# Weights cast by GpSimd's DMAs instead of VectorE, with deeper pools and a new assignment of copies to engines, in an attention and channel-mix kernel

## The chip, the cores and the metric

One core of a Trainium2 chip. The time is the device time of one execution in microseconds (us). The kernel before takes 171.91 us (median of 3 runs, 171.80 to 172.16); in the later calls, on other chips, its median was 172.37 to 172.44.

## The reference

Windowed attention with four sink tokens, then a channel mix with a shift by one token:

```python
q, k, v: (4, 8, 768, 64) float32          # batch, heads, tokens, head size
keep = is_sink | ((rel >= 0) & (rel < 128))
a = softmax(where(keep, q @ k.T / 8, -1e9));  x = (a @ v)  # -> (4, 768, 512)
x_prev = x shifted by one token
xk = mu_k * x + (1 - mu_k) * x_prev;   xr = mu_r * x + (1 - mu_r) * x_prev
k = max(xk @ w_k, 0)          # w_k 512 x 1024
v = (k * k) @ w_v             # w_v 1024 x 512
out = v / (1 + exp(-(xr @ w_r)))   # w_r 512 x 512, all float32
```

## The kernel before

The work is cut in 12 units of 256 tokens. A unit loads k, q and v, casts them to bf16, transposes k and q (on TensorE, or for later units by DMA), does scores, exponentials, mask, values, then xk and xr, then the products with wk, wr and wv. Every operation is put in a list; each engine runs its operations in a fixed order (`ORDER`), which a search has tuned. Where the plan expects TensorE to be idle for over 0.3 us at the start it puts filler products ("warm") in. They are instructions like any other and run even when the data come sooner. In the profile's lines ks, qs and vs are the loaded fp32 tiles of k, q and v; kb, qb and vb their bf16 casts; kt and qt the transposes; sc the scores and e their exponentials; rl the relu and kk its square; ob the output tile that a store reads; bank a PSUM tile.

All large transfers go through the one queue of the sync engine (SP), in order: inputs, weights, stores and DMA transposes. Weights arrive in fp32; VectorE casts them (and halves wv):

```python
LOADS = ("kq0", "v0", "kq1", "wka", "v1", "wkb", "wr", "wva", "wvb")   # order of the first loads
...
wk32 = tile1([128, NC, Dff], FP32, "wk32")        # and wr32, wv32
...
P.op("SP", 1000.0, lambda: nc.sync.dma_start(out=dst, in_=src), rank, ...)      # load_weight
...
P.op("DVE", dve(1024, 0.52), (lambda: nc.vector.tensor_scalar(        # cast: 10 of them
    out=out, in0=in_, scalar1=0.5, scalar2=None, op0=ALU.mult)) if half else
    (lambda: nc.vector.tensor_copy(out=out, in_=in_)), ...)
...
for name in ("ks", "qs", "vs"):
    pool(name, 3, [128, 2, H, D] if name == "vs" else [128, H, 2, D], FP32)
KD = range(4, 12); QD = range(8, 12)     # units whose k, q are transposed by DMA
```

The softmax here doesn't subtract the row's maximum and nothing guards it: scores larger than these inputs give would overflow.

Of the kernel before, what the change touches and what calls it, by code (L numbers as in the profile page):

```python
# [8 lines left out]
FP32 = mybir.dt.float32  # L9
# [8 lines left out]
CAST = {"k": "ACT", "q": "ACT"}  # L18

CAST0 = {"k": "DVE", "q": "DVE"}  # L20
EVAC0 = {"k": "ACT", "q": "DVE", "x": "ACT"}

KD = range(4, 12)
QD = range(8, 12)
# [11 lines left out]
LOADS = ("kq0", "v0", "kq1", "wka", "v1", "wkb", "wr", "wva", "wvb")  # L36
WCAST = ("DVE",) * 10
VCAST = ("DVE", "POOL")
# [6 lines left out]
        92, 89, 98, 105, 95, 116, 108, 113, 128, 141, 124, 119, 131, 137, 103, 148, 134, 157,  # L45
        155, 168, 219, 211, 207, 212, 220, 208, 160, 176, 165, 171, 183, 189, 215, 193, 200,
        223, 180, 216, 225, 237, 298, 186, 290, 302, 291, 303, 299, 294, 248, 295, 227, 235,
        231, 263, 232, 228, 260, 306, 266, 318, 240, 256, 245, 251, 310, 276, 269, 311, 283,
        326, 329, 308, 321, 314, 343, 315, 370, 378, 352, 366, 371, 379, 332, 367, 374, 382,
        337, 375, 384, 359, 348, 386, 396, 387, 421, 390, 274, 444, 391, 452, 445, 453, 426,  # L50
        407, 448, 456, 394, 449, 457, 460, 399, 464, 404, 465, 415, 462, 410, 430, 472, 499,
        578, 437, 468, 474, 504, 469, 525, 583, 526, 537, 485, 538, 533, 509, 529, 534, 530,
        477, 553, 482, 488, 493, 545, 511, 564, 518, 549, 541, 546, 543, 550, 601, 609, 605,
        602, 556, 610, 606, 567, 631, 613, 561, 572, 614, 617, 587, 619, 621, 594, 629, 622,
        634, 625, 639, 626, 642, 677, 689, 678, 681, 663, 690, 682, 645, 707, 685, 650, 686,
        695, 701, 670, 718, 705, 702, 693, 697, 710, 698, 760, 715, 761, 756, 768, 757, 769,
        721, 726, 764, 742, 765, 772, 749, 740, 784, 780, 774, 781, 795, 834, 830, 835, 842,
        831, 787, 843, 838, 792, 798, 860, 776, 803, 816, 839, 777, 823, 846, 848, 854, 858,
        855, 871, 910, 918, 906, 911, 907, 850, 863, 851, 919, 868, 936, 874, 914, 879, 915,
        930, 892, 924, 899, 931, 926, 947, 934, 922, 944, 939, 927, 976, 972, 977, 984, 973,  # L60
        985, 950, 980, 955, 958, 981, 988, 990, 965, 992, 996, 993, 997, 1012, 1000, 1013, 1004,
        1001, 1005, 1008, 1016, 1009, 1020, 1018, 1021, 1028, 1024, 1029, 1025,
    ),
    "DVE": (
        70, 91, 88, 93, 97, 71, 94, 99, 100, 107, 112, 101, 123, 109, 114, 110, 118, 115, 120,
        125, 143, 121, 126, 146, 144, 78, 145, 150, 79, 151, 152, 81, 164, 154, 104, 159, 147,
        175, 170, 161, 80, 162, 177, 166, 178, 167, 172, 153, 173, 82, 83, 202, 195, 196, 210,
        69, 197, 203, 204, 198, 206, 84, 85, 205, 199, 214, 218, 239, 293, 301, 222, 86, 305,
        87, 255, 297, 250, 233, 244, 229, 241, 242, 257, 246, 247, 252, 258, 253, 325, 320, 278,
        312, 279, 285, 280, 287, 322, 286, 327, 323, 328, 331, 316, 281, 289, 288, 282, 354,  # L70
        333, 334, 336, 369, 373, 338, 355, 339, 377, 361, 381, 362, 356, 363, 388, 275, 357,
        392, 364, 365, 398, 358, 403, 447, 451, 414, 455, 400, 459, 401, 409, 405, 406, 466,
        416, 417, 411, 412, 432, 433, 434, 439, 441, 440, 435, 470, 442, 481, 476, 528, 436,
        510, 487, 492, 478, 532, 479, 483, 443, 489, 484, 494, 490, 495, 540, 555, 560, 513,
        536, 514, 520, 516, 515, 522, 521, 547, 551, 523, 571, 517, 566, 557, 558, 604, 524,
        568, 569, 562, 563, 573, 574, 608, 633, 612, 616, 589, 592, 590, 638, 623, 635, 591,
        596, 598, 597, 627, 636, 640, 641, 593, 599, 644, 600, 665, 649, 646, 680, 692, 647,
        684, 651, 652, 714, 666, 688, 709, 672, 667, 674, 703, 668, 675, 673, 711, 725, 699,
        712, 676, 716, 720, 669, 717, 722, 723, 727, 759, 728, 763, 744, 767, 745, 751, 771,
        746, 753, 752, 741, 786, 782, 747, 755, 791, 797, 788, 789, 833, 793, 799, 802, 794,  # L80
        800, 748, 804, 845, 805, 754, 837, 778, 841, 825, 818, 821, 819, 820, 826, 829, 827,
        867, 856, 862, 822, 878, 909, 864, 873, 865, 852, 913, 869, 870, 875, 876, 880, 828,
        881, 917, 921, 894, 943, 897, 932, 895, 938, 896, 901, 905, 902, 945, 903, 940, 941,
        928, 949, 946, 954, 904, 951, 952, 898, 956, 975, 957, 960, 979, 961, 963, 987, 962,
        983, 967, 969, 970, 968, 971, 994, 964, 998, 1003, 1007, 1015, 1011, 1022, 1030, 1026,
    ),
    "ACT": (
        67, 68, 90, 111, 106, 96, 122, 117, 127, 130, 136, 142, 129, 132, 133, 149, 138, 163,
        135, 158, 156, 169, 174, 221, 213, 182, 209, 188, 184, 190, 201, 194, 179, 185, 224,
        181, 217, 226, 238, 187, 243, 292, 262, 300, 304, 296, 254, 249, 236, 264, 259, 265,  # L90
        261, 307, 267, 319, 268, 324, 277, 270, 284, 342, 340, 309, 330, 335, 344, 345, 347,
        353, 372, 380, 368, 420, 425, 383, 376, 360, 498, 418, 349, 385, 397, 422, 503, 423,
        402, 496, 454, 427, 446, 413, 450, 395, 458, 408, 461, 501, 577, 582, 575, 463, 431,
        473, 500, 438, 579, 475, 480, 505, 584, 527, 486, 491, 535, 531, 539, 559, 554, 512,
        519, 565, 580, 542, 544, 653, 570, 655, 603, 611, 607, 657, 632, 615, 618, 588, 659,
        637, 630, 620, 731, 595, 735, 643, 648, 679, 664, 691, 683, 729, 713, 708, 687, 671,
        696, 733, 808, 724, 706, 694, 719, 806, 762, 810, 758, 770, 743, 766, 812, 750, 785,
        790, 775, 773, 801, 882, 796, 836, 832, 844, 866, 861, 840, 817, 824, 849, 847, 884,
        859, 888, 886, 872, 877, 912, 908, 942, 920, 916, 893, 937, 925, 900, 935, 948, 923,
        953, 978, 974, 986, 959, 989, 982, 991, 966, 1014, 1002, 1006, 1010, 1019, 1017,  # L100
    ),
    "POOL": (
        77, 72, 73, 75, 76, 74, 102, 139, 140, 191, 192, 271, 273, 272, 350, 351, 428, 506, 429,
        585, 507, 661, 508, 586, 662, 737, 738, 739, 814, 815, 890, 891,
    ),
    "SP": (
        1, 3, 0, 2, 4, 5, 6, 7, 8, 11, 9, 10, 16, 12, 15, 13, 20, 14, 19, 17, 18, 21, 22, 25,
        23, 234, 24, 30, 341, 28, 35, 346, 313, 29, 317, 26, 33, 27, 389, 38, 34, 40, 31, 419,
        424, 36, 393, 497, 230, 32, 502, 37, 41, 43, 576, 39, 467, 44, 45, 581, 46, 47, 656, 42,
        548, 51, 654, 471, 52, 660, 658, 49, 552, 628, 57, 50, 48, 55, 56, 53, 730, 732, 736,  # L110
        58, 734, 54, 704, 61, 807, 811, 809, 813, 63, 700, 783, 64, 624, 62, 883, 59, 60, 885,
        889, 887, 857, 65, 853, 779, 66, 929, 933, 999, 995, 1023, 1031, 1027,
# [4 lines left out]
class Plan:  # L117
# [17 lines left out]
    def op(self, engine, cost, emit, rank, reads=(), writes=(), take=(), hold=(), port=False,  # L135
           lag=None, service=0.0, descs=128, mode=0):
        self.ops.append(dict(engine=engine, cost=cost, emit=emit, rank=rank, reads=list(reads),
                             writes=list(writes), take=list(take), hold=list(hold), port=port,
                             lag=90.0 if lag is None else lag, service=service, descs=descs, mode=mode))

    def schedule(self):
# [42 lines left out]
        while any(lines.values()):  # L184
# [35 lines left out]
            if o["service"]:  # L220

                descs = o["descs"]
# [9 lines left out]
                flying.append((dma, descs))  # L232
# [39 lines left out]
def kernel(  # L272
# [14 lines left out]
    nc = tc.nc  # L287
# [21 lines left out]
    for name in ("ks", "qs", "vs"):  # L309
        pool(name, 3, [128, 2, H, D] if name == "vs" else [128, H, 2, D], FP32)  # L310
    pool("kb", 3, [128, 2, H, D], BF16)
    pool("qb", 3, [128, 2, H, D], BF16)
    pool("kt", 4, [128, NP, 2, 128], BF16)
    pool("qt", 3, [128, NP, 2, 128], BF16)
    pool("e", 5, [128, 2, 512], BF16)
    pool("es", 3, [128, 256], BF16)
    pool("rec", 6, [128, 2, 2, 1], FP32)
    pool("x", 3, [128, 2, Dm], BF16)
    pool("td", 3, [128, 2, 256], BF16)
    pool("xk", 3, [128, NC, 256], BF16)  # L320
    pool("xr", 3, [128, NC, 256], BF16)
    pool("kk", 2, [128, NF, 256], BF16)
# [85 lines left out]
    for u in range(2, U):  # L408
        load(u, "kqv", -90 if u == 2 else 10 * u - 18)
# [521 lines left out]
```

## Time and profile before

| | before |
|---|---|
| time, median | 171.91 us |
| TensorE (PE) busy | 161.4 us of a span of 169.9 (95%) |
| VectorE (DVE), ScalarE (ACT), GpSimd (POOL) busy | 149.4, 132.5, 25.1 us |
| first product with wk / wr / wv starts | 21.30 / 28.79 / 36.85 us |

The first products mark the end of the head: from 36.85 on TensorE has all it needs. The "body" below is the stretch from the first wv product to the start of the last group of products (164.80 in this kernel, so 127.95 us). The timeline of the sync engine's issues shows the head's order of transfers (start, time until the next issue, engine and line, what, count):

```profile
8.21 2.38 SPq L397 DMA_DIRECT2D wk<-in_moe_w_k_dram  x2
10.64 4.65 SPq L360 DMA_DIRECT2D vs<-in_v_dram  x2
15.33 3.32 SPq L377 DMA_DIRECT2D qs<-in_q_dram  x1
18.69 1.82 SPq L397 DMA_DIRECT2D wr<-in_moe_w_r_dram  x1
21.25 1.51 SPq L397 DMA_DIRECT2D wv<-in_moe_w_v_dram  x1
24.02 4.44 SPq L397 DMA_DIRECT2D wv<-in_moe_w_v_dram  x1
```

The reader is to see that wk goes ahead of v of unit 1, but wr and wv go behind it: one queue, in the order in which the data are wanted. The landings follow: v of unit 1 at about 22, wr at 26.8.

### The profile page before, as it was taken

The numbers are of one execution on the slowest core, as the hardware profiler recorded it, in microseconds if no ns is written. First come the engines' busy times: TensorE is split into PE (matmuls) and PEld (weight loads), VectorE is DVE, ScalarE is ACT, GpSimd is POOL, SyncE is SP. The second block draws the span as 40 slices with busy tenths as digits, with TensorE's granted clock in tenths as the row PEclk, the third lists the DMA queues.
The fourth block names the chain that finished last, engine by engine and source line by source line (L and its number), as shares of the span: only waits on it lengthen the run. The fifth ranks groups of instructions, "written<-read, shape, count | busy, mean of one in ns | idle before, by whom it ended". The sixth has DMA issues, their size and how long they took to land.

```text
span 169.9 us, 4214 instructions
## 1 busy us (share of the span) xinstructions
PE 161.4 (95%) x1603; PEld 107.9 (63%) x1624; DVE 149.4 (88%) x372; ACT 132.5 (78%) x219; POOL 25.1 (15%) x47
## 2 busy tenths in 40 slices
PE   7898998999999999999999999999999999999992
PEld 2445575675768567768567677577585775684751
DVE  2588999999899788899999999998999999999632
ACT  3179987999999999999878979978887938654330
POOL 6130030006200030124201200110200403000000
PEclk9999999999999999999999999999999999999999
DMA  4999999999959899999858998999989974030203
GB/s 113 254 283 385 277 279 342 353 268 211 287 142 222 228 254 254 172 234 192 208 130 121 268 233 199 227 115 233 164 237 169 186 215 130 0 127 0 112 11 123
DMA packets 82803, 33.82 MB, mean 199 GB/s; under 512 B 64736, under 2 KB 77280, under 8 KB 82784
## 3 DMA queue, kind: packets, MB, share of 16 engines
q1 hardware_dynamic: 81728, 33.56, 86.8%
q8 instruction: 12, 0.20, 0.5%
q10 hardware_dynamic: 1056, 0.00, 0.3%
q14 instruction: 7, 0.06, 0.1%
HBM read 24.12 MB, written 6.29 MB: 179 GB/s over the span
## 4 chain that ended last, share of the span: by engine, by line
PE 81%; DVE 6%; DMA 5%; SPq 4%; issue 1%; ACT 1%; DVEq 0%
PE bank L818 24%; PE bank L859 23%; PE bank L841 12%; PE sc L635 6%; PE bank L694 6%; DMA wk<-in_moe_w_k_dram 5%; PE bank L733 3%; SPq L377 3%; PE bank L550 2%; PE bank L682 2%; PE bank L611 2%; SPq L360 1%; DVE e L671 1%; DVE wk_sb L503 1%; PE bank L788 1%
## 5 line engine op out<-in xcount | busy, mean ns | idle before, releaser
L818 PE MATMUL bank<-xk,wk_sb 128*128 128x256 bf16 x384 | 48.9, 273 | 0.0
L657 ACT ACTIVATE e<-sc 128x1024 bf16<-128x1024 f32 (+1 forms) x48 | 45.0, 975 | 4.9 <-PE sc L635 4.9
L859 PE MATMUL bank<-wv_h,kk 128*128 128x512 bf16 x173 | 45.3, 379 | 0.6
L818 PEld LDWEIGHTS <-wk_sb 128*128 128x128 bf16 x384 | 35.7, 98 | 7.1 <-issue 0.2
L575 POOL CAST vb<-vs 128x512 bf16<-128x512 f32 x22 | 18.4, 845 | 111.4 <-DMA vs<-in_v_dram 101.4
L827 ACT ACTIVATE rl<-bank 128x512 bf16<-128x512 f32 x48 | 27.6, 608 | 9.1 <-PE bank L818 8.4
L671 DVE TENSOR_TENSOR e<-e,mask 128x1024 bf16<-128x1024 bf16 (+1 forms) x48 | 31.6, 669 | 0.4 <-ACT e L657 0.4
L859 PEld LDWEIGHTS <-kk 128*128 128x128 bf16 x184 | 16.6, 98 | 14.7 <-DVE kk L831 0.3
L841 PE MATMUL bank<-wr_sb,xr 128*128 128x512 bf16 x88 | 23.9, 379 | 0.8 <-DVE wr_sb L503 0.4
L831 DVE TENSOR_TENSOR kk<-rl 128x512 bf16<-128x512 bf16 x48 | 20.9, 447 | 4.1 <-ACT rl L827 3.9
L768 DVE SCALAR_TENSOR_TENSOR xr<-td,mu,xt 128x256 bf16<-128x256 bf16 x48 | 23.2, 499 | 0.1
L768 DVE SCALAR_TENSOR_TENSOR xk<-td,mu,xt 128x256 bf16<-128x256 bf16 x48 | 22.3, 491 | 0.2
L710 DVE TENSOR_TENSOR x<-bank,rec 128x256 bf16<-128x256 f32 x48 | 19.5, 417 | 0.6
L694 PE MATMUL bank<-vb,e 128*128 128x65 bf16 x352 | 18.9, 193 | 0.4 <-DVE e L671 0.4
L694 PEld LDWEIGHTS <-e 128*128 128x128 bf16 x352 | 16.7, 97 | 2.8 <-DVE e L671 0.6
L847 ACT ACTIVATE th<-bank 128x512 f32<-128x512 f32 x24 | 14.1, 602 | 5.0 <-PE bank L841 4.8
L868 DVE SCALAR_TENSOR_TENSOR ob<-th,bank 128x512 f32<-128x512 f32 x23 | 15.7, 682 | 2.1 <-ACT th L847 1.7
L744 ACT COPY xt<-bank 128x512 bf16<-128x512 bf16 x24 | 14.1, 592 | 4.1 <-PE bank L733 3.8
L841 PEld LDWEIGHTS <-xr 128*128 128x128 bf16 x96 | 9.0, 98 | 8.2 <-issue 0.4
L635 PE MATMUL sc<-qt,kt 64*128 64x128 bf16 (+1 forms) x256 | 14.0, 238 | 0.0
L879 PE MATMUL bank<-warm 128*128 128x512 bf16 x42 | 12.3, 423 | 1.4 <-DVE warm L894 1.3
L635 PEld LDWEIGHTS <-kt 64*128 64x128 bf16 x256 | 8.9, 94 | 6.1 <-issue 3.7
(54 smaller groups left out, 158.5 us busy)
## 6 DMA issues: line engine op xcount, KB each, us to landing
vs<-in_v_dram SPq DMA_DIRECT2D x24, 256.0 KB, 5.0
out_dram<-ob SPq DMA_DIRECT2D x23, 256.0 KB, 3.4
ks<-in_k_dram SPq DMA_DIRECT2D x18, 256.0 KB, 4.9
qs<-in_q_dram SPq DMA_DIRECT2D x7, 512.0 KB, 6.2
qs<-in_q_dram SPq DMA_DIRECT2D x10, 256.0 KB, 4.1
wk<-in_moe_w_k_dram SPq DMA_DIRECT2D x2, 1024.0 KB, 8.7
wv<-in_moe_w_v_dram SPq DMA_DIRECT2D x2, 1024.0 KB, 12.3
ks<-in_k_dram SPq DMA_DIRECT2D x3, 512.0 KB, 8.1
```

Source lines behind the costliest of these rows:

```text
L575: lambda g=g, copy=copy: copy(out=buf["vb", u][:, g, :, 0:D], in_=buf["v", u][:, g, :, :]), rank,
L635: nc.tensor.matmul(out=sc[:, a, o0:o1], lhsT=lhs[rows], rhs=rhs[rows], start=True, stop=True)
L657: nc.scalar.activation(out=buf[ek][:, :, lo:], in_=buf[sck][:, :, lo:], func=AF.Exp, scale=scale)
L671: nc.vector.tensor_tensor(out=at, in0=at, in1=m, op=ALU.mult)
L694: nc.tensor.matmul(out=o[:, g, a, :], lhsT=e[:, a, e0:e0 + 128], rhs=rhs, start=(T == 0 and i == 0), stop=(i == len(blocks) - 1), skip_gro ...
L710: P.op("DVE", dve(256), lambda ok=ok, rk=rk, c=c: nc.vector.tensor_tensor(out=buf["x", u][:, :, 128 * c:128 * c + 128].rearrange("p g (a d ...
L768: nc.vector.scalar_tensor_tensor(out=buf[key][:, c0 + i, :], in0=buf[tk][:, i, :], scalar=mu[w][:, c0 + i:c0 + i + 1], in1=xt[:, c0 + i, t ...
L818: nc.tensor.matmul(out=ps[:, i, :], lhsT=wk_sb[:, c, 128 * f:128 * f + 128], rhs=xk[:, c, :], start=(c == 0), stop=(c == NC - 1), skip_gro ...
L827: P.op("ACT", act(512), lambda psk=psk, rk=rk: nc.scalar.activation(out=buf[rk], in_=buf[psk].rearrange("p (i t) -> p i t", i=2), func=AF. ...
L831: P.op("DVE", dve(512, 0.52), lambda f2=f2, rk=rk: nc.vector.tensor_tensor(out=buf["kk", u][:, 2 * f2:2 * f2 + 2, :], in0=buf[rk], in1=buf ...
L841: nc.tensor.matmul(out=buf[psk], lhsT=buf["xr", u][:, c, 128 * g:128 * g + 128], rhs=wr_sb[:, c, :], start=(c == 0), stop=(c == NC - 1))
L859: nc.tensor.matmul(out=buf[psk], rhs=wv_h[:, f, :], lhsT=buf["kk", u][:, f, 128 * g:128 * g + 128], start=(f == 0), stop=(f == NF - 1))
```

## The change

The intent: GpSimd's DMAs cast fp32 to bf16 on the way, so the casts of wk and wr on VectorE go away, and the fp32 copies of the weights with them (40 KB of each partition, which deeper pools take). Then the assignment of copies to engines and all orders were searched anew.

```diff
-LOADS = ("kq0", "v0", "kq1", "wka", "v1", "wkb", "wr", "wva", "wvb")
-WCAST = ("DVE",) * 10
+LOADS = ("kq0", "v0", "kq1", "v1")
+WLOADS = (("wk", 0, 2, ("q", 0, 1)), ("wk", 2, 4, ("v", 0, 1)), ("wr", 0, 2, ("k", 1, 1)),
+          ("wv", 0, 2, ("k", 1, 1)), ("wv", 2, 4, ("q", 1, 1)))   # each behind this landing
-QD = range(8, 12)
+QD = range(6, 12)
+CHOICE = {80: "DVE", ...}     # some 60 casts, evacuations, relus: which engine
 ...                           # ORDER: all five lists new
-        P.op("SP", 1000.0, lambda: nc.sync.dma_start(out=dst, in_=src), rank, service=service,
+        def emit():
+            t = buf[what, u]
+            t = t[0:1, part, 0, 0:1] if what == "v" else t[0:1, 4 * part, 0, 0:1]
+            nc.gpsimd.tensor_copy(out=gate[0:1, n:n + 1], in_=t)
+            nc.gpsimd.dma_start(out=dst[cut], in_=src[cut])
 ...
-        pool(name, 3, [128, 2, H, D] if name == "vs" else [128, H, 2, D], FP32)
-    pool("kb", 3, ...); pool("qb", 3, ...); pool("qt", 3, ...); pool("e", 5, ...)
+        pool(name, 4, [128, 2, H, D] if name == "vs" else [128, H, 2, D], FP32)
+    pool("kb", 4, ...); pool("qb", 4, ...); pool("qt", 4, ...); pool("e", 6, ...)   # and others
-    for i in range(4): cast(i, wk_sb..., wk32...)      # and 2 of wr, 4 of wv
+    # only wv is halved, in place, in bf16
```

The copy of one element into `gate` is what makes each weight DMA wait for an input.

## The prediction

> **What bounds the kernel now.** I read the page first: busy shares and the slices, then the chain that ended last.
>
> ```profile
> span 169.9 us, 4214 instructions
> ...
> PE 161.4 (95%) x1603; PEld 107.9 (63%) x1624; DVE 149.4 (88%) x372; ACT 132.5 (78%) x219; POOL 25.1 (15%) x47
> ...
> PE   7898998999999999999999999999999999999992
> ...
> DVE  2588999999899788899999999998999999999632
> ...
> PE 81%; DVE 6%; DMA 5%; SPq 4%; issue 1%; ACT 1%; DVEq 0%
> ```
>
> The reader is to see that TensorE is the bound, that VectorE is close behind it, and that 15% of the final chain is not TensorE: a DMA of wk and its queue (5% + 4%) and VectorE (6%). These must lie at the start, so I took the busy time of each engine in stretches.
>
> ```profile
> 0.00:5.00 5.00, 3.74 (x11) 1.43 (x12) 1.48 (x5) 1.28 (x1) 3.66 (x14) 1.00 0.58 130
> ...
> 15.00:20.00 5.00, 4.19 (x51) 2.70 (x49) 4.59 (x13) 4.95 (x9) 0.00 (x0) 1.00 1.15 324
> ...
> 80.00:100.00 20.00, 19.83 (x212) 12.81 (x211) 19.69 (x53) 16.28 (x29) 3.52 (x6) 1.00 0.85 180
> ...
> 160.00:165.00 5.00, 4.95 (x31) 2.96 (x31) 1.61 (x4) 2.57 (x6) 0.00 (x0) 1.00 0.28 105
> ```
>
> (Columns: stretch, length, then busy us of PE, PE weight load, DVE, ACT, POOL, clock, DMA share, GB/s.) In the middle PE idles under 1% and DVE is 98% busy too: both are full. From 40 to 160 PE's idle time sums to only 1.0 us. PE in the first 20 us looks busy but is not: the timeline shows what it does.
>
> ```profile
> 18.27 0.63 PE L611 MATMUL bank<-qt,ksink 128*128 128x256 bf16 x4
> 18.95 1.72 PE L879 MATMUL bank<-warm 128*128 128x512 bf16 x7
> 20.61 0.76 PE L635 MATMUL sc<-qt,kt 64*128 64x256 bf16 x12
> 21.30 2.79 PE L818 MATMUL bank<-xk,wk_sb 128*128 128x256 bf16 x24
> ```
>
> The warm products are filler. The channel-mix product with wk, the first dense work, starts at 21.30. Real PE work, by the spacing of back-to-back products in the chain (0.109 us for a 256-column one, 0.216 for 512): 384+16 products of 256 columns 43.6, 184+96 of 512 columns 60.4, scores about 10, values with sinks about 14, sink scores 3.5, the 48 groups of four transposes at 0.22 10.6, sink values 0.8: **143 us**. Before 21.30 only some 5 us of it is done (8 groups of transposes, two units' scores, one unit's values). So the time is 21.3 (start) + 145.4 (to the last products at 166.7; 138 of work, some 4.5 of the 0.1 us steps around each group of scores, 2.4 of visible idle) + 3.2 (last eviction and store).
>
> **What sets 21.3** is in the chain in order of time:
>
> ```profile
> 8.21 7.76 DMA wk<-in_moe_w_k_dram
> ...
> 16.01 0.75 DVE x L710 x2
> ...
> 17.55 0.60 DVE wk_sb L503
> 18.16 0.39 DVE xk L768
> ...
> 18.89 0.59 DVE wk_sb L503
> ...
> 19.80 0.48 DVE xk L768
> 20.28 0.60 DVE wk_sb L503
> ```
>
> VectorE ends attention of unit 0, then makes xk and casts wk by turns: 3 x 0.60 = 1.8 us of casts lie on the path, and earlier 1.8 us of memsets (7.83 to 9.7 in its timeline) sit ahead of the second k cast at 9.64.
>
> **What the Trainium skill says.** (1) "DMA: Bandwidth & Descriptors", SWDGE vs HWDGE vs iDMA: a cast during DMA is only possible from GpSimd. So moving weights to that queue is what removes the casts; no run here shows it yet. (2) The same page, Issuing engines are not separate DMA queues: all issuers share 16 engines. The trace agrees in kind: everything but the two mu loads goes through one queue and fills the engines (1.15 of 1 as the view counts it at 15 to 20 us), so the 5 MB of weights still compete with the inputs. (3) "SBUF — State Buffer", SBUF: two separate sides: VectorE in a two-port mode locks GpSimd out, and descriptors for GpSimd's DMAs then come late. The trace has only casts on GpSimd to compare: 0.85 us mean for 128x512, between 0.61 and 1.07, while VectorE is full. (4) "VectorE: DVE Perf Modes", the perf-mode tier table: bf16 copies in SBUF are faster than fp32 ones, and PSUM sources are capped. Agrees: a 128x512 cast in SBUF 0.42, a PSUM copy of the same size 0.72; so halving wv in bf16 should cost less than the 0.687 it costs from fp32. My estimate is 0.35.
>
> **The change part by part.**
>
> *Weight path.* Removed from VectorE: 6 casts x 0.60 spacing = 3.6 us, of which 1.8 lies on the path to 21.3; 4 halvings drop from 0.60 to about 0.28: 1.3. In exchange GpSimd issues five DMAs, each after one landed input. In its order they stand behind a v cast and the sink keys, which need unit 0's kt (before: 11.35 to 12.0). So wk leaves about 10 to 12 us, against 8.21 and 9.4 before, where landing took 7.9 and 9.5. wk lands, I estimate, at 17 to 20 (first half), so it may just meet xk.
>
> *Head order.* Loads now go k, q, q, k; unit 0's first pair is complete with the second landing, not the third (6.4 us in the trace), and the memsets come before the casts. I estimate first scores 0.5 to 1 us sooner than 8.21 and the second pair 1.5 us sooner than 11.34. Against that, VectorE's order puts three more PSUM copies of unit 1 (0.62 each by spacing) before xk, and v's second half queues behind all of k of unit 1. Net with the 1.8 us of casts: the first wk product 1 to 3 us sooner, at **about 19.3**. The instruction lists support it: 44 fillers become 29. At 0.21 us each that is 3.2 us less of gaps that the author's order expects.
>
> *PE.* q of units 6 and 7 is transposed by DMA: 4 groups less, 4 x 0.22 = **0.9 us** off the bound, and 2 more groups come before the first wk product (0.4). Cost: 4 more DMA transposes (3.3 us to landing, hidden).
>
> *VectorE, ACT, GpSimd.* Counting the lists: ACT loses 17 casts of k and q, 10 evacuations, 2 xt and 5 relus, and gains 10 v casts: 17x0.53 + 10x0.65 + 7x0.5 - 10x0.5 = 14 us less. VectorE gains 7 k/q casts and 6 v casts (13x0.35), 8 evacuations and transposed copies (8x0.62) and 5 relus (5x0.6): 12.5 us more, less the 4.9 above: **+7.6**, so some 157 us busy. About 5 of the gains are in the first 20 us, where it has 6.3 us idle. GpSimd swaps 16 v casts for 10 k/q casts: less work. So in the middle VectorE's load stays near 128 of 135 us, since 6 weight operations leave and about 7 us come. It stays full; I book no gain and no loss.
>
> *Deeper pools.* They can only take PE's 2.4 us of visible idle, and most of that is waits on VectorE or ACT at 24 to 30. I book **0.5**.
>
> Sum: 2.0 (start) + 0.9 + 0.5 + about 0.4 (two more groups done early) = 3.8 off 171.9: **168.1**; rounded to **168.0**.
>
> **The rivals.**
> 1. *The weights come late.* The program order on PE is fixed, so if wk lands at 22 or wv after 37 (the first wv product before is at 37.29) PE stands still. For it: they share the engines with a sync queue that, with four buffers, runs further ahead; the queue moves 250 to 350 GB/s, and 5 MB of weights plus 5 MB of inputs for the first units are needed by about 36 us, some 33 us of traffic. GpSimd's issue may be locked out by VectorE. Against: only half as many bytes are written to SBUF, and the weights have a queue to themselves. It would make 170 to 174.
> 2. *VectorE becomes the bound.* 157 us busy in a span of 166, with 4 at the start and 7 at the end that cannot be used, leaves nothing. For it: 98% busy from 80 to 100 and 120 to 140. Against: the moved copies sit mostly at the head. It would eat the transposes' and pools' gains: 169 to 170.
> 3. *The head gains all that the fillers suggest* (3 to 4 us), and early gaps between 24 and 30 (1.5 us) close as casts leave VectorE there: 165 to 166.5.
>
> **Range and chances.** Rival 3 gives the low end, 165.2; rivals 1 and 2 mildly the high end, 171.2. The 2% line is 168.47, close to my sum. The change is evidently a re-tuned whole, so I lean a little to the side of gain: faster 0.57, within 2% 0.38, slower 0.05.
>
> **What would show it.** First wk product: about 19.3 (right between 18.3 and 20.3). Filler products about 28. VectorE about 157 us busy, ACT about 117, PE's busy time 155 to 158. PE's idle from 21 to 160 at most 2.5 us; a wait of over 1 us of PE on a DMA of wk, wr or wv shows rival 1. VectorE over 97% in every stretch from 30 to 140 with PE idle beside it shows rival 2. I would be wrong above all if landing of GpSimd's DMAs takes over 12 us, or if the input loads of units 1 and 2 are pushed back by the weights so that xk comes no sooner.

## The result, and the profile after

The changed kernel takes 183.76 us (median of 4 runs, 180.84 to 185.64) against 172.03 in the same rounds. The ratio of the fast runs is 1.059 (95% interval 1.0457 to 1.0723). Ratios here are always the mean time of one kernel's fast runs over that of the other's fast runs in the same rounds, so they are not quite the ratios of the medians. A run over 1.5% above the fastest run of the same kernel is counted as slow and left out of the ratios; that leaves two of these four. The profiled execution is the slowest, 185.64 us, and counts as slow; the waits of the head that are read from it below were found again in e1, whose profiled run (183.35) is fast and which differs by one early move only.

The page of the changed kernel: busy shares, TensorE in 40 slices, its granted clock, and the chain that ended last.

```profile
PE 163.6 (89%) x1573; PEld 107.4 (58%) x1593; DVE 155.0 (84%) x393; ACT 120.6 (66%) x195; POOL 25.6 (14%) x51
...
PE   7885744979899999999999999999999798999992
...
PEclk9999678699999999999999999999999999999999
...
PE 39%; DMA 24%; DVE 18%; SPq 12%; ACT 3%; issue 3%; DVEq 0%
```

TensorE has holes in slices 4 to 7 (14 to 32 us) and thin ones near 140 to 160; its share of the final chain fell from 81% to 39%, and transfers with their queue are 36% of it. VectorE's 155.0 and ScalarE's 120.6 are near the predicted 157 and 117. What TensorE did in the head, from its timeline (in brackets the idle time just before, and who ended it):

```profile
21.98 0.28 PE L830 MATMUL bank<-xk,wk_sb 128*128 128x256 bf16 x1
...
25.50 3.47 PE L830 MATMUL bank<-xk,wk_sb 128*128 128x256 bf16 x15 [3.24 <-DVE xk L780]
...
31.87 0.30 PE L704 MATMUL bank<-vb,e 128*128 128x65 bf16 x4 [2.66 <-ACT vb L581]
...
46.41 1.04 PE L879 MATMUL bank<-wv_h,kk 128*128 128x512 bf16 x4 [0.58 <-DVE kk L852]
```

The first wv product comes at 46.41 instead of 36.85: 9.6 us of the loss lie before it. Two views name the transfers: GpSimd's timeline, where DMA_DIRECT2D is the issue of a weight DMA, and the chain in order of time (start, length, what).

```profile
10.48 0.88 POOL L416 DMA_DIRECT2D wk_sb<-in_moe_w_k_dram  x1
...
12.97 0.74 POOL L416 DMA_DIRECT2D wr_sb<-in_moe_w_r_dram  x1
...
14.68 0.74 POOL L416 DMA_DIRECT2D wv_h<-in_moe_w_v_dram  x1
```

```profile
11.72 19.46 DMA vs<-in_v_dram
...
31.20 0.62 ACT vb L581
```

All five weight DMAs leave between 10.48 and 14.68. wk lands after 7.6 and 9.8 us, wr after 12.2, wv after 14.7 and 17.4. And the second half of v of unit 1, issued at 11.72 on the sync queue, about when it was before (11.52), takes 19.46 us and lands at 31.2, nine microseconds later than before (22.2).

The body is 132.1 us (46.41 to 178.52) against 127.95, although TensorE has less to do there. So there are two losses, some 9 to 10 us in the head and some 4 in the body; in the fast run of e1 the body (45.88 to 176.37) is 130.5, so that some 2.5 of these 4 are seen in a fast run. The experiments take the two losses one by one.

### The profile page after: what moved, and what is told of

It is laid out like the page before. It is cut to its first block, busy times and chain, and to the rows that moved or that the text cites. A ratio compares the mean times of both kernels' runs of the same rounds, so it can differ in the third digit from the quotient of the medians.

```text
span 183.7 us, 4162 instructions
## 1 busy us (share of the span) xinstructions
PE 163.6 (89%) x1573; PEld 107.4 (58%) x1593; DVE 155.0 (84%) x393; ACT 120.6 (66%) x195; POOL 25.6 (14%) x51
## 4 chain that ended last, share of the span: by engine, by line
PE 39%; DMA 24%; DVE 18%; SPq 12%; ACT 3%; issue 3%; DVEq 0%
DMA vs<-in_v_dram 16%; PE bank L879 13%; PE bank L830 11%; DMA out_dram<-ob 5%; PE bank L861 4%; SPq L389 4%; DVE xr L780 3%; PE bank L704 3%; DVE e L681 3%; SPq L382 3%; SPq L546 3%; SPq L372 2%; DVE xk L780 2%; DMA kt<-kb 2%; PE sc L645 2%
## 5 line engine op out<-in xcount | busy, mean ns | idle before, releaser
L830 PE MATMUL bank<-xk,wk_sb 128*128 128x256 bf16 x384 | 52.3, 277 | 5.8 <-DVE xk L780 4.0
L667 ACT ACTIVATE e<-sc 128x1024 bf16<-128x1024 f32 (+1 forms) x48 | 44.3, 960 | 3.6 <-PE sc L645 3.5
L840 ACT ACTIVATE rl<-bank 128x512 bf16<-128x512 f32 x43 | 24.8, 603 | 12.8 <-PE bank L830 7.4
L681 DVE TENSOR_TENSOR e<-e,mask 128x1024 bf16<-128x1024 bf16 (+1 forms) x48 | 30.1, 636 | 0.1
L704 PE MATMUL bank<-vb,e 128*128 128x65 bf16 x352 | 20.0, 197 | 2.9 <-ACT vb L581 2.7
L704 PEld LDWEIGHTS <-e 128*128 128x128 bf16 x352 | 17.5, 100 | 6.7 <-issue 4.0
L852 DVE TENSOR_TENSOR kk<-rl 128x512 bf16<-128x512 bf16 x48 | 18.9, 414 | 0.8 <-ACT rl L840 0.8
L752 ACT COPY xt<-bank 128x512 bf16<-128x512 bf16 x22 | 13.0, 589 | 8.4 <-PE bank L743 4.3
L692 PE MATMUL bank<-vsink,es 128*128 128x130 bf16 x64 | 13.0, 227 | 0.8 <-ACT rl L840 0.6
L717 DVE RECIPROCAL rec<-bank 128x4 f32<-128x4 f32 x48 | 7.6, 172 | 5.5 <-PE bank L704 5.3
```

Of the source, the lines that this page charges most:

```text
L667: nc.scalar.activation(out=buf[ek][:, :, lo:], in_=buf[sck][:, :, lo:], func=AF.Exp, scale=scale)
L681: nc.vector.tensor_tensor(out=at, in0=at, in1=m, op=ALU.mult)
L704: nc.tensor.matmul(out=o[:, g, a, :], lhsT=e[:, a, e0:e0 + 128], rhs=rhs, start=(T == 0 and i == 0), stop=(i == len(blocks) - 1), skip_gro ...
L830: nc.tensor.matmul(out=ps[:, i, :], lhsT=wk_sb[:, c, 128 * f:128 * f + 128], rhs=xk[:, c, :], start=(c == 0), stop=(c == NC - 1), skip_gro ...
L840: nc.scalar.activation(out=buf[rk], in_=buf[psk].rearrange("p (i t) -> p i t", i=2), func=AF.Relu)
L852: P.op("DVE", dve(512, 0.52), lambda f2=f2, rk=rk: nc.vector.tensor_tensor(out=buf["kk", u][:, 2 * f2:2 * f2 + 2, :], in0=buf[rk], in1=buf ...
```

## The experiments

Eighteen experiments were run (e1 to e19; there is no e11). Except where said, buffers, plan and orders are those of the kernel that each starts from; only the named operation moves. All results are correct but those of e12, e13 and e14, which are wrong on purpose.

**The head: which of three things made it late?** The candidates: A, the weights' transfers crowd out the inputs; B, mu_k is loaded late (ScalarE issues it at 11.78, and VectorE waits 2.61 us for it); C, TensorE's clock falls (0.66 to 0.83 from 15 to 35 us).

*e1_mu_first.* Changed kernel, mu_k's load (operation 69) moved to the front of ScalarE's order, ahead of operation 70.

```diff
+        for i, there, after in [(69, 70, 0)]:
+            line.remove(i)
+            line.insert(line.index(there) + after, i)
```

> The changed kernel with one move: ScalarE issues the load of mu_k first instead of after unit 0's second v cast (11.8 us, landing 9.0 us later). Theory A (the five weight DMAs, all issued between 10.5 and 15 us, crowd out the inputs of unit 1, whose v lands at 31.2 us): xk's first piece comes 2 to 3 us sooner (about 18.3 instead of 20.9), but the next pieces stand behind the cast of unit 1's v in VectorE's order, so the first long run of wk products still starts at 25 to 26 us and the time stays within 1.5 us of the changed kernel's (181 to 185). Theory B (late mu_k is the cause): the first wk products 3 us sooner, and the time 3 us or more lower (178 to 180).

182.99 us (182.43 to 183.35), ratio 1.061 (1.0582 to 1.0637). The first wk product came at 20.28, but the rest waited 4.49 us for xk, whose later pieces stand on VectorE behind the cast of v of unit 1. The first wv product came at 45.88. Mending mu_k only showed the next wait: B is no cause by itself.

*e2_weights_late.* Changed kernel, wr and wv issued only after unit 1's v has landed.

```diff
+            if name != "wk":
+                what, u, part = "v", 1, 1
```

> The changed kernel, where the DMAs of wr and of both halves of wv wait for the landing of unit 1's second v half instead of k and q of unit 1; nothing else changes. Theory A (crowding): unit 1's v lands by about 20 to 22 us instead of 31.2, PE's wait of 2.7 us for its cast goes, the first wv product comes 5 to 8 us before 46.4, and the time falls to 174 to 178. Theory B (mu_k): v lands sooner, but the first run of wk products starts hardly before 24, and the time stays above 180. Theory C (PE's granted clock of 0.66 to 0.83 between 17 and 34 us is the cost): the clock recovers only as far as PE's gaps close, so it can't be told from A here; the run with fillers tells.

176.77 us (176.53 to 178.41), ratio 1.0272 (1.0224 to 1.0321). The two halves of v landed at 22.1 and 23.3 instead of 24.6 and 31.2, the first wv product came at 39.01. Three DMAs leaving some 12 us later (wr at 24.94 instead of 12.97) gave back 6 to 7 us: A is shown.

*e3_both.* The two edits together.

> Both edits together. Theory A with B as a part: the first long run of wk products starts at 19 to 21 us, the first wv product at 35 to 38, and the time is 169 to 174, 9 to 13 us less than the changed kernel's; what remains over 168 is the loss later in the kernel (3 to 4 us between 100 and 160 us, where the sync queue's stores and loads come late). If the head is not the cause at all, the time stays at 181 to 185.

176.59 us (175.20 to 179.10), ratio 1.0212 (1.0149 to 1.0275): as e2; the expected 169 to 174 was missed. TensorE still waited 4.15 us for xk behind the v cast.

*e4_fillers.* Changed kernel with 32 more filler products, to keep TensorE's clock up.

```diff
+EXTRA = {("prep", 2, "q", 0): 8, ("kp", 0, 0, 0): 14, ("o", 1, 1): 10}
```

> The changed kernel with 32 more filler products (8 before unit 2's q transposes, 14 before the first wk product, 10 before unit 1's third group of values), which wait for nothing but the bank that the next product needs. Theory C (the lowered clock costs much of the loss): the granted clock stays at 0.95 or more from 15 to 35 us and the time falls by 3 us or more (178 to 180). Theory A: the clock rises too, but the waits on landings stay, the first long run of wk products still starts at 25 to 26 us, and the time falls by less than 2 us.

184.76 us (184.73 to 187.09), ratio 1.0749 (1.0685 to 1.0812). The clock was full up to 30 us and 0.66 from 30 to 35, where the changed kernel has 0.66 to 0.83 from 15 to 35; the first wv product came at 47.59 and the time did not fall. The wait for v of unit 1 was still there (3.42 us). Fourteen fillers stand right ahead of the first wk product, which came at 23.69, so they may cost something themselves; but a full clock until 30 us bought nothing: C falls as the cause.

*e7_v_cast_after_xk.* e3, and the v cast moved behind xk on VectorE.

```diff
+        for i, there, after in [(69, 70, 0), (135, 148, 1)]:
```

> The changed kernel with mu_k first and wr, wv behind unit 1's v (the run with both edits), and in VectorE's order the cast of unit 1's first v half moved from the middle of xk to behind it. In the run with both edits PE waits 4.2 us for xk behind that cast. Theory E (the order of work, which lets PE's next dense run stand behind a landing, is what remains of the head's loss): the first long run of wk products starts at 20 to 21.5 instead of 24.4 us, a part of the wait comes back as a wait for values, and the time falls by 1 to 3 us against the run with both edits (173 to 175). If instead the landing of v itself is the limit, the wait only moves to the values and the time falls by less than 1 us.

176.01 us (175.19 to 176.80), ratio 1.0203 (1.0152 to 1.0254). TensorE's timeline of e7:

```profile
19.91 1.92 PE L836 MATMUL bank<-xk,wk_sb 128*128 128x256 bf16 x16 [0.55 <-DMA wk_sb<-in_moe_w_k_dram]
25.33 0.27 PE L698 MATMUL bank<-vsink,es 128*128 128x130 bf16 x1 [3.49 <-DVE vsink L614]
```

The wk products now start at 19.91, close to the predicted 19.3, and it is worth under 1 us: the wait moved to the values, which need v of unit 1.

**The same path in the kernel before.** Four kernels put only the weight path into the kernel before, with its own orders, and differ in when the DMAs leave.

*e5_before_gps_spaced.* Weights by GpSimd's casting DMAs, wr and wv behind the cast of v of unit 1; the six casts on VectorE are gone.

```diff
-        P.op("SP", 1000.0, lambda: nc.sync.dma_start(out=dst, in_=src), rank, service=service,
+            nc.gpsimd.tensor_copy(out=gate[0:1, n:n + 1], in_=t)
+            nc.gpsimd.dma_start(out=dst, in_=src)
+    BEHIND = {"wka": ("k", 0, 1), "wkb": ("v", 0, 0), "wr": ("v", 1, 1), "wva": ("v", 1, 1),
+              "wvb": ("v", 1, 1)}
```

> The kernel before, with one part of the change: the weights are loaded and cast by GpSimd DMAs (6 casts on VectorE gone, wv halved in bf16), all orders and buffers otherwise as before. wk leaves behind the first landings, and wr and wv only after GpSimd has cast unit 1's v (about 23 us), so near the times that they left at before. Theory A (only the crowding of inputs by weights that leave too early hurts): unit 1's v lands within 2 us of before's 22, the first wk product stays at 20 to 22 us, and the time is 169.5 to 173. Theory D (the GpSimd path is itself slow, by late descriptors or slow transfers): wk takes over 11 us to land, the first run of wk products starts after 23 us, and the time is above 174.

176.65 us (174.49 to 177.13), ratio 1.0199 (1.0128 to 1.027), above the 169.5 to 173 of theory A. Neither theory had it: the second half of v of unit 1 is in time at 22.2, but wr is now late (issued at 23.24, before at 18.69), and TensorE waits for it (this profiled run counts as slow; e8, a fast one, has the same wait at 3.1 us):

```profile
32.33 1.04 PE L856 MATMUL bank<-wr_sb,xr 128*128 128x512 bf16 x3 [3.69 <-DMA wr_sb<-in_moe_w_r_dram]
```

*e6_before_gps_together.* The same, wr and wv right behind wk, as the change has it.

```diff
-[(8, 74, 0), (11, 74, 0), (14, 140, 1), (13, 140, 1), (12, 140, 1)]
+[(8, 74, 0), (11, 74, 0), (12, 139, 0), (13, 139, 0), (14, 139, 0)]
```

> As the spaced run, but wr and both halves of wv leave right behind wk (behind k and q of unit 1), as in the changed kernel; nothing else differs. Theory A: unit 1's v lands 3 to 9 us later than in the spaced run, PE waits for its cast, and the time is 4 to 9 us above the spaced run. Theory D: both runs within 1.5 us of one another.

179.20 us (178.81 to 179.87), ratio 1.0393 (1.0363 to 1.0423); one wait of TensorE of 6.42 us at about 26. wr landed after 11.6 us and wv after 14.2 and 17.1, as in the changed kernel. The input that came late here was not the expected one: v of unit 1 landed at 23.88 (22.23 in e5), but q of unit 2 at 31.14 (24.04 in e5), and ScalarE, which had the cast of it next in its order, did not come to the relu that TensorE waited for. The loss against e5 (2.6 us by the medians) is less than the 4 to 9 expected.

*e9_before_gps_paced.* wr leaves when q of unit 1 has landed, wv after unit 1's v.

```diff
-[(8, 74, 0), (11, 74, 0), (14, 140, 1), (13, 140, 1), (12, 140, 1)]
+[(8, 74, 0), (11, 74, 0), (12, 139, 0), (14, 140, 1), (13, 140, 1)]
```

> The kernel before with all weights cast by GpSimd's DMAs, as in e5, but wr is issued as soon as q of unit 1 has landed (about 18 us instead of 23.24) and wv after unit 1's v. Theory A (what costs is when the weights' transfers leave against the inputs, not the path itself): PE's wait for wr (3.69 us in e5) falls under 1 us and the time is 171.5 to 174. Theory D (whatever the times of issue, the second queue takes from the inputs what it gives to the weights): wr lands at 27 to 28, but v of unit 1 or k and q of unit 2 land later by as much, and the time stays at 175 to 178. Theory H of the prediction (six casts less on VectorE are worth up to 2 us when the weights are in time): under 171.

173.70 us (173.01 to 174.51), ratio 1.0075 (1.0048 to 1.0103). TensorE no longer waits for wr, and the first wv product comes at 38.03. wr left at 14.26, earlier than expected and near e6's 13.74; what separates e9 from e6 is that the halves of wv left at 25.45 and 26.31 instead of 14.75 and 15.61. q of unit 2 landed at 26.42. So e6, e5 and e9, which do the same work, take 179.2, 176.7 and 173.7 us by the moments at which three DMAs leave alone. That is A in its clearest form: which input is hit depends on what is in flight. Theory H, that six casts fewer would gain, fails too: at its best the new path is 1.3 us slower than casting on VectorE.

*e8_before_gps_pools.* e5 with the deeper pools.

```diff
-        pool(name, 3, [128, 2, H, D] if name == "vs" else [128, H, 2, D], FP32)
+        pool(name, 4, [128, 2, H, D] if name == "vs" else [128, H, 2, D], FP32)
```

(and one more buffer in kb, qb, qt, e, td, xk, xr, kk, rl, ob and vb)

> The spaced run with the deeper pools of the change, orders as before. If the pools are worth what was booked for them, 0.5 us or less below the spaced run; if sync's queue running further ahead of the weights costs landings, the first wv product comes later and the time is 1 us or more above the spaced run.

176.48 us (176.28 to 177.39), ratio 1.0248 (1.0211 to 1.0285), where e5 had 1.0199: with these orders the deeper pools are worth nothing that can be seen.

**Why do fewer operations on VectorE not shorten the head?**

*e10_before_memsets_early.* The kernel before, the 1.8 us of memsets first on VectorE.

```diff
+        for i, there, after in [(71, 70, 1)]:
```

> The kernel before with one move only: the memsets of sinks, ones columns and shift columns (1.8 us on VectorE between 7.83 and 9.7) run before the first casts instead of between them. The prediction counted this among the 1 to 3 us that the first wk product was to come sooner. If the head's order on VectorE sets the first wk product: it comes 0.5 to 1.8 us before 21.30, and the time is 170 to 171.5. If the landing of the inputs sets it: within 0.3 us of 21.30 and 172 to 172.6.

172.38 us (172.03 to 172.86, 13 runs), ratio 0.9998 (0.9987 to 1.0009): nothing, to a tenth of a per cent. The first wk product came at 21.80, the first wv product at 37.48. (On this chip the first k landed at 6.94, 0.5 us later than in the profile of before, so 21.80 here stands for 21.30 there.) One explanation was that the fillers hold TensorE whenever data come sooner; two kernels without fillers after the first 8 us test it.

*e17_paced_memsets_no_fill* (e9 with the memsets first) and *e18_before_memsets_no_fill* (e10):

```diff
-    P.fill_until = 45000.0
+    P.fill_until = 8000.0
```

> e9 (weights by GpSimd's DMAs at their time, no casts of wk and wr; 173.7) with the memsets of e10 first and no filler products after the first 8 us of the plan. In e9 and e10 the same fillers stand in TensorE's order whether or not data come sooner. Theory F (the fillers hold the head: what the casts and memsets free is only seen without them): first wk product at 19 to 20.5 (22.0 in e9), and the time 171 to 172.8. Theory T (later landings, of v of unit 1, wr and unit 2, set the next wait): first wk product sooner, but the first wv product at 37.5 to 38.5 as in e9, and 173 to 174.5. If TensorE, left without fillers, is granted a lower clock that costs: PEclk under 0.9 after 15 us and over 174.5.

> e10 (the kernel before with the memsets first; 172.38) without filler products after the first 8 us of the plan. Theory F: first wk product at 20 to 21 (21.80 in e10), 170.8 to 172. Theory T: the first wk product sooner, the first wv product as in e10 (37.5), 172 to 173. If the clock falls and costs: over 173.

e17 173.85 us (173.39 to 174.83), ratio 1.0093 (1.006 to 1.0127). e18 172.59 us (171.62 to 175.07, 22 runs, in two clusters near 172.3 and 174.3 that stay unexplained), ratio 1.0015 (0.9992 to 1.0038). Without the fillers the first wk product came no sooner, at 22.56 in both: theory F has no support. The timeline of e17 shows what is ahead of it:

```profile
21.35 0.40 PE L650 MATMUL sc<-qt,kt 64*128 64x256 bf16 x6 [0.98 <-ACT kt L575]
22.23 0.40 PE L650 MATMUL sc<-qt,kt 64*128 64x256 bf16 x6 [0.49 <-ACT e L672]
22.56 2.79 PE L833 MATMUL bank<-xk,wk_sb 128*128 128x256 bf16 x24
```

In the old order the second pair of scores of unit 1 stands ahead of the first wk product, and it waits for ScalarE: for the evacuation of kt and for the exponentials of the first pair. VectorE's xk had been done (at 19.8 in e5). The clock fell to 0.50 in these kernels from 15 to 20 us, and twelve scores took 1.03 us where e9 has 0.61, so the test is not clean; the medians moved by 0.2 us or less. The profile of the kernel before, with fillers and a full clock, shows the same tie. The end of VectorE's third cast, and ScalarE's exponential of the first pair:

```profile
20.20 0.69 DVE L503 CAST wk_sb<-wk 128x1024 bf16<-128x1024 f32 x1
```

```profile
19.88 1.04 ACT L657 ACTIVATE e<-sc 128x1024 bf16<-128x1024 f32 x1
```

The cast ends at 20.89, the exponential at 20.92; the last six scores start at 20.97, released by ScalarE, and the wk product follows at 21.30. The three casts lay on the chain that the profile printed, but beside them ran a chain through ScalarE that was as long.

**How much is the traffic?** Three kernels load no weights at all.

*e12_no_weight_traffic.* Changed kernel, each weight DMA replaced by a memset on GpSimd.

```diff
-            nc.gpsimd.dma_start(out=dst[cut], in_=src[cut])
+            nc.gpsimd.memset(dst[cut], 0.0078125)
```

> The changed kernel with the five weight DMAs replaced by memsets on GpSimd in the same places (wrong result on purpose), so that no weight byte moves. Theory A (the weights' traffic at the head is the whole loss): v of unit 1 lands before 24, the first wv product comes before 38.5, and the time is 168 to 172. Theory L (the re-planned orders also lose by themselves later, by the order of loads, stores and transposes on the sync queue): PE's idle time from 100 to 160 stays over 2 us, and the time is 173 to 177. If the weights don't matter: 180 or more.

175.70 us (174.96 to 176.02), ratio 1.0181 (1.0157 to 1.0206). It is not clean: the memsets kept GpSimd busy from 10 to 20 us, and beside them five instructions of VectorE took 4.88 us, so that TensorE was busy for only 2.44 of the 5 us from 10 to 15.

*e13_before_no_weights.* The kernel before without weight loads, casts of wk and wr replaced by memsets on VectorE.

```diff
-        P.op("SP", 1000.0, lambda: nc.sync.dma_start(out=dst, in_=src), rank, service=service,
+        P.op("SP", 1000.0, lambda: None, rank, service=service,
-                (lambda: nc.vector.tensor_copy(out=out, in_=in_)), rank, reads=reads,
+                (lambda: nc.vector.memset(out, 0.0078125)), rank, reads=reads,
```

> The kernel before with the weight loads taken out and its casts of wk and wr replaced by memsets (wrong result on purpose), as what e12 is to be measured against: VectorE keeps ten operations on weights, no weight byte moves. Theory A: the head gets shorter, as inputs come sooner: 168 to 171, and e12 is within 2 us of it. Theory L: e12 is slower than this one by over 3 us. If the head of the kernel before is not limited by its transfers at all: within 0.5 us of 172.

173.46 us (173.21 to 174.06), ratio 1.0055 (1.0036 to 1.0073). Without any weight traffic the kernel before gets no faster, where 168 to 171 was expected by theory A. The run is not clean either: its memsets take 0.91 us each where the casts took 0.69, TensorE waits 0.74 us for one, and the first wk product comes 1.0 us later than in e10 (22.78 against 21.80). That one ordered queue hides the weights fully fits this run, but is not shown by it.

*e14_no_weights_clean.* e12 made clean: all products read one small tile, filled once.

```diff
-            nc.gpsimd.dma_start(out=dst[cut], in_=src[cut])
+            if n in (0, 2, 3):
+                nc.gpsimd.memset(w0 if n == 0 else wk_sb[:, n - 2, 0:512], 0.0078125)
-                                         lhsT=wk_sb[:, c, 128 * f:128 * f + 128],
+                                         lhsT=w0[:, 128 * (f % 4):128 * (f % 4) + 128],
```

(and `w0` in place of wr_sb and wv_h)

> The changed kernel without its weight DMAs, made cleaner than e12: e12's five memsets kept GpSimd busy from 10 to 20 us and slowed VectorE beside them (5 instructions in 4.88 us). Here every product reads its weights from one 128x512 tile filled once (wrong result on purpose), three memsets of 512 columns take the place of five DMAs. Theory A (the weights' traffic at the head is nearly the whole loss of 11.7 us): 172 to 174, the first wv product before 37.5. Theory L (the new orders lose 3 to 4 us in the body by themselves): 174 to 176.5, with 129.5 us or more from the first wv product to the last group of products (128 in the kernel before).

173.67 us (173.38 to 174.40), ratio 1.0077 (1.0055 to 1.01). Its first products, from the timeline:

```profile
19.28 2.73 PE L832 MATMUL bank<-xk,w 128*128 128x256 bf16 x16
...
35.39 1.04 PE L881 MATMUL bank<-w,kk 128*128 128x512 bf16 x4 [0.23 <-DVE kk L854]
```

The changed kernel without its weight traffic starts its wk products at 19.28, as predicted, and its first wv product comes 2.1 us sooner than e10's 37.48. Its body, 35.39 to 166.56, takes 131.2 us against e10's 128.2 (37.48 to 165.68). Both are in the total: 2.1 won, 3.0 lost, 1.3 slower in the medians (173.67 against 172.37). The traffic itself costs what the changed kernel takes above this: 182.2 us, the mean of its two fast runs, less 173.7 is 8.5 us, or 10.1 from the medians.

**The body: VectorE full, or the sync queue?** In e7 the body had some 2 us of visible idle time of TensorE. (The profiles of before, after, e7 and some others lack about 20 matmul records, 1573 of 1593 in e7. In before and e7 that shows as 16 or 17 even gaps of 0.05 us from 40 to 160, some 0.9 us in all that is no idle time. e10, whose records are complete, has 0.0 us of idle time there where before has 0.9; e7's is then about 1.2.)

*e15_vector_to_scalar.* e7 with the 23 copies and relus that the change had given to VectorE after the head back on ScalarE (the expectation says 24; the traces count 23 on both engines).

```diff
-                self.ops[i]["emit"]()
+                alts = self.ops[i]["alts"]
+                back = i > 150 and self.ops[i]["engine"] == "DVE" and alts and "ACT" in alts
+                (alts["ACT"][1] if back else self.ops[i]["emit"])()
```

> e7 (weights late, mu_k first, v cast behind xk; 176.01) with the 24 casts, evacuations and relus that the change moved to VectorE after the head given back to ScalarE, in their places. Rival 2 of the prediction (VectorE is the bound of the body: 19.3 to 19.6 us busy of 20 in e7): VectorE's busy time falls by about 12 us and the time to 173.5 to 175. Theory Q (the sync queue's order of loads, stores and transposes loses the time in the body): within 0.7 us of 176. If ScalarE now holds the body up: over 177.

179.26 us (178.62 to 181.93), ratio 1.0392 (1.036 to 1.0424): 3 us slower than e7, though VectorE's busy time fell from 151.8 to 146.3 us (its profiled run counts as slow). Taking load off VectorE did not help, but ScalarE's busy time rose from 120.2 to 132.2 us, and over 177 is what was expected if ScalarE then holds the body up. So this run alone does not settle whether VectorE was the bound; e16 does. Moving the copies to VectorE was right, given the new order.

*e16_stores_by_gpsimd.* e7 with the 23 whole stores on GpSimd's queue.

```diff
-                nc.sync.dma_start(out=out[b, s0:s0 + 128, :], in_=buf[bk])
+                nc.gpsimd.dma_start(out=out[b, s0:s0 + 128, :], in_=buf[bk])
```

> e7 (176.01) with the 23 whole stores issued by GpSimd instead of the sync queue, so that no load and no transpose stands behind a store that waits for its ob. Theory Q (the sync queue's order): the waits for DMA of vs, ks and kt on the chain shrink, and the time is 173.5 to 175. Rival 2 (VectorE is full): within 0.7 us of 176. If GpSimd's issuing of 0.74 us each disturbs VectorE or its own casts: over 177.

174.28 us (173.12 to 177.15; 6 of 9 runs fast), ratio 1.0087 (1.0061 to 1.0114). The table by stretches, first e7, then e16 (stretch, length, busy us of TensorE, weight load, VectorE, ScalarE, GpSimd, clock, DMA share, GB/s):

```profile
120.00:140.00 20.00, 19.48 (x175) 12.48 (x177) 18.65 (x46) 15.38 (x26) 1.84 (x4) 1.00 0.95 217
140.00:160.00 20.00, 19.24 (x202) 12.96 (x202) 18.33 (x49) 11.18 (x19) 0.61 (x1) 1.00 0.47 100
```

```profile
120.00:140.00 20.00, 20.00 (x210) 13.75 (x210) 19.16 (x50) 14.38 (x24) 4.66 (x10) 1.00 1.07 228
140.00:160.00 20.00, 19.73 (x192) 13.44 (x190) 18.43 (x47) 11.11 (x18) 3.75 (x6) 1.00 0.27 72
```

TensorE's idle time from 60 to 160 falls from 1.92 us (some 1.2 without the missing records) to 0.28, while VectorE stays as full as it was: so it is not VectorE's load that bounds TensorE here. What went away is a wait of VectorE: from 40 us on it waited for a store to free an ob tile for 2.8 us in the changed kernel, 2.0 in e14, 0.9 in e7, and not at all in e16 or in the kernel before. A store that leaves late on the sync queue keeps its tile, VectorE stands before it, and TensorE behind VectorE: in e14 the longest idle time of TensorE in the body, 0.78 us, ends with such an ob. Of the 2.1 us between the two profiled runs (1.7 between the medians; different chips) 0.8 lie in the body; 1.6 lie ahead of the first wv product, where no store runs yet, and may be chance.

*e19_before_q67_by_dma.* The kernel before with one part of the change alone: q of units 6 and 7 transposed by DMA. Operations keep their places; each new transpose goes onto the sync queue just ahead of k's of the same half unit.

```diff
-QD = range(8, 12)
+QD = range(6, 12)
```

> The kernel before with only one part of the change: q of units 6 and 7 is transposed by DMA, so that TensorE loses 4 groups of four transposes (4 x 0.22 = 0.9 us by the prediction) and ScalarE 4 evacuations; the sync queue gains 4 transposes of 1.2 us and 2 loads. If the prediction's term is right and the body is bound by TensorE: 171.2 to 171.8 against 172.4 (ratio 0.993 to 0.997). If the longer sync queue makes loads or transposes late, as theory Q found for the changed kernel: 172.2 to 174, with waits of TensorE on kt, qt or v between 70 and 120 us.

175.18 us (174.63 to 176.14), ratio 1.0173 (1.0144 to 1.0203): not 0.9 us faster but 2.7 slower, more than either theory expected. Its table by stretches and TensorE's timeline:

```profile
80.00:100.00 20.00, 18.08 (x194) 11.84 (x194) 18.80 (x48) 15.27 (x26) 5.84 (x7) 1.00 1.08 198
```

```profile
81.32 0.28 PE L696 MATMUL bank<-vb,e 128*128 128x65 bf16 x4 [1.05 <-POOL vb L577]
```

TensorE, busy for 19.83 us in this stretch of the kernel before, is busy for 18.08. Each DMA transpose holds the in-order sync queue for about 1.2 us, so the loads of v behind it leave later (the one at the root of this wait at 75.00, its counterpart in the kernel before at 72.11), GpSimd casts v later (79.13 against 76.24), and TensorE waits for it. The four transposes had been counted as hidden because their own landing is early enough; it is the loads behind them that are late. With another order of the queue it might do better; that was not tried.

No kernel here beats the kernel before. e10 equals it, and e18 cannot be told from it.

## Why the prediction was wrong

The prediction said 168.0 us (165.2 to 171.2) with 0.05 for slower; it is 183.76. By its own steps:

1. **"The first wk product 1 to 3 us sooner", at about 19.3,** is the step that failed: it is a sum of operations on VectorE and GpSimd, and takes the landings of the inputs as given. It came at 21.98 for one product and 25.50 for the others. The size of the gain was right where the traffic is away: 19.28 in e14, 19.91 in e7. And wk's own landing, estimated at 17 to 20 for the first half, was 18.1. What was missing is what the other three weight DMAs do to v of unit 1: landing at 31.2 instead of 22.2. The text says that the weights "still compete with the inputs", cites that all issuers share the engines, works out "33 us of traffic" that are needed by about 36 us, and names as its worst case "the input loads of units 1 and 2 are pushed back by the weights". But it put this aside with "only half as many bytes are written" and "the weights have a queue to themselves", and gave the rival 170 to 174. The first reason does not hold here: the source bytes came at about the same pace. By 21 us e3 had moved 4.37 MB as counted (208 GB/s), of which up to 1.05 MB is wk counted at half its source size, so up to 5.4 MB of source, an estimate; the kernel before had moved 5.50 MB (262 GB/s). The second reason is the cause itself: a queue of its own takes its share at once, whatever the other queue needs first (e6, e5, e9: 179.2, 176.7, 173.7).
2. **"1.8 us of casts lie on the path", 1.8 us of memsets:** not gained in the kernel before (e9, e10: 0). The reading of the printed chain was right; a second chain through ScalarE's kt and exponentials was as long (20.92 against 20.89 us in the kernel before; e17, e18).
3. **0.9 us off the bound by four groups of transposes:** alone it is +2.7 us (e19). "Hidden" was checked for the landing of the transposes (3.3 us), not for the 1.2 us that each takes from the in-order queue.
4. **Deeper pools, 0.5:** nothing seen (e8). **Two groups earlier, 0.4:** not tested by itself.
5. **VectorE and ScalarE:** predicted 157 and 117 us busy, measured 155.0 and 120.6; fillers predicted 28, recorded 28; halving wv predicted 0.35, measured 0.414 us (0.687 from fp32). These were nearly right, and the time does not depend on them. TensorE's busy time of 155 to 158 was wrong (163.6). Products at a low clock count as busy for longer (15 wk products took 3.47 us, where 24 took 2.79 before), but that is a part only: e14, at a full clock, has 161.4. The 2.4 us of visible idle time that the prediction counted are in part missing records (0.9 us from 40 to 160). Two readings were off: the first wv product before is at 36.85, not 37.29, and GpSimd's casts took 0.61 to 1.69 us, not 0.61 to 1.07; nothing in the sum rests on them.
6. **Rivals:** rival 1 is what happened, at several times its size: it had no term for a fixed order in which TensorE, VectorE and ScalarE all stand behind one late input. Rival 2 falls (e16; e15 does not settle it). Rival 3's head gain exists only without weight traffic (e14).

In sum, from e14 against e10: head 2.1 us shorter, body 3.0 longer, and 8.5 to 10.1 us of traffic on top. That a longer sync queue costs time in the body is shown for the kernel before (e19); for the changed kernel e16 and the waits for ob point to the same, with 0.8 us of the body in one profile each. Left open: in e14 the body has 2.2 us of visible idle time from 40 to 160 (e10 has none), so about a third of the 3.0 us is in steps between products that the profile counts as busy; and why the best pacing, e9, still costs 1.3 us.

## What to carry to other kernels

When transfers fill the engines, one queue in order of need is a schedule, and a second queue is a second claim on the same engines: before moving loads to it, list for each early microsecond which bytes must have landed, and hold the others back until then. A chain that the profile prints is one of several nearly equal ones; before booking a gain from it, look at what else the next product in the engine's fixed order waits for. For work moved onto an in-order DMA queue, count what it delays behind it, not only when it lands.

## What the Trainium skill lacked or had wrong

- "DMA: Bandwidth & Descriptors", Queues, rings and completion order, says that each engine takes packets from its queues in turn. The runs agree with it and show the size, which the page does not give: five weight DMAs on a second queue within 4.2 us made a load of v on the first take 19.46 us instead of about 11, and took 7.6 to 17.4 us themselves.
- The same page, the fit for GpSimd's DMAs in Anatomy of one DMA (about 2.0 us plus bytes over 436e3 per us), gives for a 1 MB source an estimate of 4.4 us, and its table in Bandwidth 6.15 us for 1 MB. With the engines shared no weight DMA here came under 6.7 us (wr in e16). The page has the figure for one DMA alone, and none for one that shares the engines with another queue's transfers.
- The same page, SWDGE vs HWDGE vs iDMA, says that a cast needs GpSimd, not whether the halved destination saves time. Here it saved none: wk landed after 7.6 and 9.8 us with the cast, 7.9 and 9.5 without.
- The same page, DMA Transpose (X-bar), says that the plain form must be issued from SP or ACT. That section has no time for what one costs the issuing queue: about 1.2 us each here, and four more of them 2.7 us of the whole time (e19).
- "SBUF — State Buffer", SBUF: two separate sides, warns that VectorE can keep descriptors of GpSimd's DMAs waiting. No run here shows it: the issues took 0.74 to 0.88 us each beside a nearly full VectorE. The other direction was seen: beside GpSimd's 1.79 us memsets in e12 one cast of VectorE lasted 3.43 us, which took 0.86 in e14.
